# Twelve of sixteen score products ahead of V, and two-row runs for wo's heads 24 to 29, in a gated mix of cached attention and a SwiGLU block

## The chip, the cores and the metric

The kernel runs on one core of a Trainium2 chip. The core has a matrix engine (TensorE, PE in the profile; its weight loads are PEld), a vector engine (VectorE, DVE), a scalar engine (ScalarE, ACT), a general engine (GpSimd, POOL) and a sync engine (SyncE, SP), which here issues nearly all transfers. Sixteen DMA engines move data between the memory of the chip and the core's on-chip memory. The metric is the device time of one execution in microseconds (us), as a median of several runs.

## The reference

One token is decoded. `x` has 512 numbers; there are 32 heads of 128 numbers, each with a cache of 65,536 keys and as many values, all in bf16.

```
q = (x @ wq) as 32 heads of 128
scores = einsum(q, k_cache) * 128 ** -0.5
p = softmax(scores)
o = einsum(p, v_cache)
a = o as 4096 numbers @ wo                     # wo: 4096 x 512
b = (silu(x @ w_gate) * (x @ w_up)) @ w_down   # 512 -> 1792 -> 512
g = sigmoid(sum(x * gate_w))
out = g * a + (1 - g) * b
```

The two caches are 537 MB each, and every byte of them is read once.

## The kernel before

**Tiles.** A tile is 128 x 128 cache rows, that is 128 partitions with `NB` = 128 rows each; rows have 128 numbers. Two tiles are a pair (64 KB a partition, 8.39 MB). A head has four tiles (`G`), two pairs (`MH`), so there are 128 tiles (`N`) and 64 pairs (`M`). There are two buffers for K pairs (`K_bufs`, a half for each tile) and one for V (`V_buf`).

**A step.** Step `m` handles K pair `m` and V pair `m-2`. A step with an even `m` is the first of a head's two, one with an odd `m` the second (`second` in the matrix engine's code, `b == 1` elsewhere).

- *Vector engine* (`vector_step`, L342). `product` (L279) multiplies the pair's first tile by the query in place. `add_once` (L309) adds the upper 64 numbers of each row to the lower 64 and raises the credit `c_S[0]`. Then comes the maximum of the previous head (`top_of`, L330) or the fold of the tile before. The second tile is multiplied, and `add_halves` (L291) adds halves down to 16 numbers, the last of them into `T_sb`, and raises `c_S[1]`. Just ahead of that last add it folds the pair's first tile: `fold` (L320) sums four columns of the score accumulator `S_ps` into `S_sb`, after waiting for the matrix engine's event `pe_S`. In a second step the other tile's fold and the row maximum (`row_max`, L326) follow.
- *Matrix engine* (`tensor_step`, L683). It takes credits, each raised by another engine, in a fixed order. `take(c_S[0])`, then 16 products of the 64 remaining columns with a unit matrix, four columns each, which accumulate into `S_ps[0]` (`scores`, L513). Then `c_P` (probabilities are ready; first steps only, in second steps it is taken ahead of the scores) and `c_V` (the V pair has landed). Then 64 products of probabilities with V into `O_ps` (`values`, L537), 32 for each tile, each tile ending with the event `pe_V`. Then the sum of the exponentials (`total`), the next query's spread (`query_spread`, L527), `c_S[1]` and the four scores of the second tile out of `T_sb`, the turn of `O_sb` (`head_turn`, L545) and the turn of the maximum (`max_turn`, L530). The first matrix product on `T_sb` raises `pe_K`, which frees the K pair.
- *Scalar engine* (`scalar_step`). It forms the exponentials into `P_sb`, copies `O_ps` out (`o_copy`), scales a head's output into `oT` (`head_out`) and copies the new query.
- *Sync engine* (`sync_step`, L214). It waits for `pe_V`, issues the next V pair's load (L181), waits for `pe_K` and issues the load of a K pair (L181). GpSimd passes on that V has landed, as the credit `c_V` (`tell_of_v`).

Steps 2 to 61 are loops on the matrix engine (two steps an iteration, 30 iterations), the vector engine (four steps) and the scalar engine (four heads, up to `GROUPED`). The last two K pairs are written out; there the scores of both tiles are 16 products, and `add_halves` stops at 64 columns.

**The end.** `sync_end` (L220) issues the last V tiles in pieces and then `wo` (`load_wo`, L187) into the first K buffer, in the pieces of `WO_CUTS`. The first 28 heads (`GROUPED`) are loaded so that a partition takes four rows of `wo` that lie side by side, a run of 4 KB; the other heads take a run of 1 KB for each head. Because of that order, `o_copy` writes a head's output in a regrouped order and `head_out` puts it into `oT` in four pieces of 32 partitions. `project` (L551) multiplies `oT` by `wo` head by head, two products a head, waiting for each piece of `wo`. The two halves of the result are then copied out by the vector and the scalar engine (L388, L392), and 1 KB is written back (L237).

Of the kernel before, what the change touches and what calls it, by code (L numbers as in the profile page):

```python
# [10 lines left out]
P = 128  # L11
NB = 128
PAIR = 2 * NB
QUAD = 4


WIDE = 64
WIDTH = 16

TURNED = 8  # L20
WO_CUTS = (0, 4, 8, 12, 16, 20, 24, 28, 30, 31, 32)
HALVES = (0, 64, NB)
LAST_CUTS = (0, 32, 64, 96, 112, NB - TURNED, NB)

GROUPED = 28


class Events:
# [12 lines left out]
def kernel(  # L41
# [18 lines left out]
    _, H, Sk, Dh = A_k_cache.shape  # L60
# [17 lines left out]
    def sb(name, shape, dtype=f32):  # L78
        return consts.tile(shape, dtype, name=name)
# [10 lines left out]
    O_sb = sb("O_sb", [4, 4 * Dh])  # L90
# [3 lines left out]
    ident_b, ones_b, q_diag = (sb(n, [P, P], bf16) for n in ("ident_b", "ones_b", "q_diag"))  # L94
# [3 lines left out]
    oT = sb("oT", [P, H], bf16)  # L98
# [12 lines left out]
    S_ps = [psum.tile([P, NB, QUAD], f32, name=f"S{i}_ps") for i in range(2)]  # L111
    O_ps = psum.tile([4, 4 * Dh], f32, name="O_ps")
# [13 lines left out]
    def halves(buf):  # L126
        return [buf[:, i * NB * Dh : (i + 1) * NB * Dh].rearrange("p (j d) -> p j d", d=Dh) for i in range(2)]

    K_half, V_half = [halves(b) for b in K_bufs], halves(V_buf)

    wo_sb = K_bufs[0][:, : H * D].rearrange("p (h n) -> p h n", n=D)

    def v_view(n):
        return {N - 4: K_half[0][1], N - 3: V_half[0], N - 2: V_half[1], N - 1: K_half[1][1]}[n]

    sync, act, dve, pool, pe = nc.sync, nc.scalar, nc.vector, nc.gpsimd, nc.tensor
# [3 lines left out]
    po, pe_x, pe_S, pe_V, pe_q, pe_m, pe_t, pe_o = (  # L140
        Events(nc, n) for n in ("po", "pe_x", "pe_S", "pe_V", "pe_q", "pe_m", "pe_t", "pe_o")
    )
# [9 lines left out]
        for n in ("x_in", "gw_in", "wq_in", "ka_in", "kb_in", "kc_in", "wg_in", "wu_in", "wd_in", "vA_in", "vB_in")  # L152
# [4 lines left out]
              for n, c in ((N - 3, HALVES), (N - 2, HALVES), (N - 1, LAST_CUTS))}  # L157
    wo_in = {a: Events(nc, f"wo{a}", 16) for a in WO_CUTS[:-1]}

# [7 lines left out]
    def wait(engine, events, value):  # L167
        key = id(engine), id(events)
        value -= taken.get(key, 0)
        if seen.get(key, 0) < value:  # L170
            engine.wait_ge(events.sem, value)
            seen[key] = value
# [10 lines left out]
    def load_tile(view, cache, n, events, a=0, b=NB):  # L183
        start = n % 2 * NB
        events(sync.dma_start(out=view[:, a:b, :], in_=rows_of(cache, n)[:, start + a : start + b, :]))  # L185

    def load_wo(a, b):  # L187
        runs = wo_sb.rearrange("p (g j) n -> p g (j n)", j=QUAD)
        rows = A_wo.rearrange("(h p) n -> p h n", p=P)
        row_runs = A_wo.rearrange("(g p j) n -> p g (j n)", p=P, j=QUAD)  # L190
        if b <= GROUPED:
            A, B = a // QUAD, b // QUAD
            wo_in[a](sync.dma_start(out=runs[:, A:B, :], in_=row_runs[:, A:B, :]))  # L193
        else:
            wo_in[a](sync.dma_start(out=wo_sb[:, a:b, :], in_=rows[:, a:b, :]))


    def load_v(i):
# [21 lines left out]
    def sync_end():  # L220
        wait(sync, pe_D, 6)
        load_tile(v_view(N - 4), A_v_cache, N - 4, v4_in)
        for n in (N - 3, N - 2, N - 1):
# [5 lines left out]
            for events, a, b in zip(end_in[n], cuts[:-1], cuts[1:]):  # L229
                load_tile(v_view(n), A_v_cache, n, events, a, b)  # L230
        for a, b in zip(WO_CUTS[:-1], WO_CUTS[1:]):
            load_wo(a, b)
# [45 lines left out]
            wait(dve, ac_q, n // G)  # L278
        return own[0](dve.tensor_tensor(out=K, in0=K, in1=q_rep, op=ALU.mult))  # L279

    def add_halves(n, width, last, out=None, ahead=None):
        K = K_half[n // 2 % 2][n % 2]
        half, mark = Dh // 2, last
        while half >= width:
            wait(dve, own[0], mark)
            to = K[:, :, 0:half]
            if half == width and ahead is not None:
                fold(ahead)
            if half == width and out is not None:
                to = out  # L290
            ins = dve.tensor_tensor(out=to, in0=K[:, :, 0:half], in1=K[:, :, half : 2 * half], op=ALU.add)  # L291
            if half == width and out is not None:
                ins.then_inc(c_S[n % 2], 1)
            else:
                mark = own[0](ins)
            half //= 2
        marks["K", n] = mark
# [16 lines left out]
    def fold(n):  # L314
        h, g = divmod(n, G)
        if n < G or n >= N - G:
            wait(dve, pe_D, n + 1 if n < G else n + 1 - N + 2 * G)
        else:
            wait(dve, pe_S, n + 1 - G)
        return own[0](dve.tensor_reduce(  # L320
            out=S_sb[h % 2][:, g * NB : (g + 1) * NB], in_=S_ps[n % 2], axis=AXIS.X, op=ALU.add
        ))
# [19 lines left out]
    def vector_step(m):  # L342
        h, b = divmod(m, MH)
        width, to = (WIDTH, T_sb) if m < M - 2 else (WIDE, None)
        last = product(2 * m)
        if to is not None:
            add_once(2 * m, last)
        if b == 0:
            top_of(h - 1)
        else:  # L350
            fold(2 * m - 1)
        if to is None:
            add_halves(2 * m, width, last)
        last = product(2 * m + 1)
        if b == 1:
            weight(h - 1, m - 1)
        add_halves(2 * m + 1, width, last, to, 2 * m)
        if b == 1:
            row_max(h, fold(2 * m + 1))

# [39 lines left out]
    def at(tile, first, i):  # L400
        return tile[:, first + i : first + i + 1] if isinstance(first, int) else tile[:, bass.ds(first + i, 1)]
# [19 lines left out]


    def o_copy(h):
        if h >= GROUPED:
            return copy(O_sb, O_ps)
        return copy(
            O_sb.rearrange("q (c j a) -> q c a j", c=4, j=QUAD),
            O_ps.rearrange("q (c a j) -> q c a j", c=4, j=QUAD),
        )


    def head_out(h, src, first=0):
        wait(act, dv_rg, h + 1)
        if h >= GROUPED:
            return copy(oT[:, h : h + 1], src, rg[:, h % 2 : h % 2 + 1])
        g, part = divmod(h, QUAD)
        A = P // QUAD
        for j in range(QUAD):
            ins = copy(
                at(oT[part * A : (part + 1) * A, :], first, g * QUAD + j),  # L440
                src[j * A : (j + 1) * A, :],
                rg[j * A : (j + 1) * A, h % 2 : h % 2 + 1],
            )
        return ins
# [42 lines left out]
    def scalar_end():  # L487
        took_rounds(act, scalar_waits, GROUPED // QUAD)
        for m in range(2 + GROUPED * MH, M):
            scalar_step(m)  # L490
# [17 lines left out]
        pe.wait_ge(credit, 1)  # L508
        pe.sem_inc(credit, -1)  # L509

    def scores(n, src, width, events, start=0, stop=NB):
        for c in range(0, width, QUAD):
            ins = pe.matmul(  # L513
                S_ps[n % 2][:, start:stop, :], lhsT=ident_b, rhs=src[:, start:stop, c : c + QUAD],
                start=(c == 0), stop=(c == width - QUAD),
            )
            if c == 0 and events is pe_S and n == 1:
                pe_K(ins)
        if stop == NB:
            events(ins)  # L520
# [14 lines left out]
    def values(probs, view, start, stop, opens, closes):  # L535
        for j in range(start, stop, 4):
            ins = pe.matmul(  # L537
                O_ps, lhsT=probs[:, j : j + 4], rhs=view[:, j : j + 4, :],
                start=(opens and j == start), stop=(closes and j == stop - 4),
            )  # L540
        return ins
# [141 lines left out]
    def tensor_step(m):  # L683
        second = m % MH
        if second:
            take(c_P)
            total()
        take(c_S[0])
        scores(0, K_half[m % 2][0], WIDE, pe_S)
        if not second:  # L690
            take(c_P)
        take(c_V)
        for i in range(2):
            pe_V(values(P_sb[:, i * NB :], V_half[i], 0, NB, i == 0, i == 1))
        if not second:
            total()
        take(c_q)
        query_spread(pe_q)
        take(c_S[1])
        scores(1, T_sb, WIDTH, pe_S)  # L700
        take(c_o)
        head_turn()
        take(c_m)
        max_turn()


    def tensor_end():
# [31 lines left out]
        for n in range(N - 3, N):  # L739
            probs = P_last[:, n % G * NB : (n % G + 1) * NB]  # L740
            cuts = LAST_CUTS if n == N - 1 else HALVES
            for events, a, b in zip(end_in[n], cuts[:-1], cuts[1:]):
                wait(pe, events, 16)
                if n == N - 1 and a == NB - TURNED:
                    break
                ins = values(probs, v_view(n), a, b, False, n == N - 1 and b == NB - TURNED)
            pe_V(ins)
            if n == N - 2:
                total(1)
        wait(pe, ac, marks["oh_read"])  # L750
        for j in range(NB - TURNED, NB):
            pe.matmul(
                oh, lhsT=v_view(N - 1)[:, j, :], rhs=probs[:, j : j + 1],
                start=(j == NB - TURNED), stop=False,
            )
        for a, b in zip(WO_CUTS[:-1], WO_CUTS[1:]):
            wait(pe, wo_in[a], 16)
# [7 lines left out]
    with tc.tile_critical():  # L765
# [6 lines left out]
        sync_out()  # L772
        with act.Fori(0, GROUPED, QUAD) as first:
            scalar_round(first)
# [45 lines left out]
```

## Time and profile before

| What | Value |
|---|---|
| median of 3 runs | 2516.11 us (2516.02 to 2516.18) |
| the profiled execution | 2517.2 us |
| its span, first to last instruction | 2515.4 us |
| mean granted matrix-engine clock | 0.774 of full |
| PE, PEld busy | 1487.4 us (59%), 616.2 us (24%) |
| DVE busy | 2003.4 us (80%) |
| ACT busy | 182.3 us (7%) |
| read from memory | 1087.64 MB, 432 GB/s over the span |

The profile was taken in one execution. Busy times overlap between engines, so they do not add up to the span. "Idle before" a group of instructions names what ended the idleness; PEq is the matrix engine's own sequencer, as when it takes a credit. Times within the span are counted from its first instruction. SPq lines show when the sync engine issued a transfer, not when data moved.

### The profile page before, as it was taken

Reading aid. Unit: us, or ns where it says so; the run is one execution under the profiler, and the core shown is the slowest. Engines: PE = TensorE matmul, PEld = TensorE weight load, DVE = VectorE, ACT = ScalarE, POOL = GpSimd, SP = SyncE. Lnnn points to the kernel's source line nnn. Section 1 sums busy time; section 2 is a strip of 40 time slices with the busy share of each in tenths; the row PEclk is TensorE's granted clock in tenths of the full one; section 3 lists DMA queues with packets and bytes.
Section 4 is the critical chain, followed back from the end, with each engine's and each line's share of the span. In section 5 each row is a group of like instructions: output and inputs, shape, how many; then the busy total and the mean of one; then the engine's idle time right before and its main releaser. Section 6 shows DMA issues by size and latency. Waiting matters only on the chain. (4 is left out here: it accounts for less than half of the span.)

```text
span 2515.4 us, 15705 instructions
## 1 busy us (share of the span) xinstructions
PE 1487.4 (59%) x6589; PEld 616.2 (24%) x6589; DVE 2003.4 (80%) x678; ACT 182.3 (7%) x503; POOL 0.7 (0%) x6
## 2 busy tenths in 40 slices
PE   2655655646556556465575565654745656547569
PEld 1322222222222222222222222222212222222223
DVE  5887887877878878779788788787787887977881
ACT  0000000000000000000000000000000000000000
POOL 0000000000000000000000000000000000000000
PEclk8777878778778777787787777877877778778789
DMA  9999999999999999999999999999999999999999
GB/s 414 438 433 436 435 434 434 434 434 434 435 434 434 434 434 434 435 436 435 435 435 434 437 434 435 435 434 437 435 434 434 434 434 434 434 435 434 434 431 387
DMA packets 22605, 1087.80 MB, mean 432 GB/s; under 512 B 2753, under 2 KB 3266, under 8 KB 4546
## 3 DMA queue, kind: packets, MB, share of 16 engines
q1 hardware_dynamic: 22306, 1087.65, 99.9%
q8 instruction: 7, 0.11, 0.0%
q10 hardware_dynamic: 288, 0.00, 0.0%
q14 instruction: 4, 0.03, 0.0%
HBM read 1087.64 MB, written 0.00 MB: 432 GB/s over the span
## 5 line engine op out<-in xcount | busy, mean ns | idle before, releaser
L279 DVE TENSOR_TENSOR K_buf<-K_buf,q_sb 128x16384 bf16<-128x16384 bf16 (+1 forms) x129 | 1112.0, 8620 | 348.8 <-DMA K_buf<-in_A_k_cache_dram 346.1
L513 PE MATMUL S_ps<-K_buf,ident_b 128*128 128x512 bf16 (+1 forms) x1104 | 388.9, 527 | 867.3 <-PEq L509 834.3
L537 PE MATMUL O_ps<-V_buf,P_sb 128*4 128x512 bf16 x3968 | 866.9, 379 | 28.6 <-PEq L509 28.3
L537 PEld LDWEIGHTS O_ps<-V_buf,P_sb 128*4 128x4 bf16 x3968 | 332.9, 85 | 560.1 <-issue 57.6
L291 DVE TENSOR_TENSOR K_buf<-K_buf 128x4096 bf16<-128x4096 bf16 (+1 forms) x127 | 433.7, 3415 | 3.1
L513 PEld LDWEIGHTS S_ps<-K_buf,ident_b 128*128 128x128 bf16 x1104 | 133.5, 126 | 1101.0 <-issue 1036.8
L309 DVE TENSOR_TENSOR K_buf<-K_buf 128x8192 bf16<-128x8192 bf16 x60 | 265.5, 4425 | 2.0
L392 ACT ACTIVATE O_sb<-O_ps 4x512 f32<-4x512 f32 x63 | 63.3, 1005 | 1705.1 <-PE qm_ps L527 1674.8
L320 DVE TENSOR_REDUCE S_sb<-S_ps 128x128 f32<-128x512 f32 x128 | 88.2, 689 | 105.4 <-PE S_ps L513 103.3
L530 PE MATMUL qm_ps<-diag,ones_f 128*128 128x128 f32 x126 | 33.5, 353 | 72.3 <-PEq L509 70.2
L545 PE MATMUL oh_ps<-ident_f,O_sb 4*128 4x1 f32 x504 | 64.3, 244 | 19.6 <-PEq L509 19.6
L291 DVE TENSOR_TENSOR T_sb<-K_buf 128x2048 bf16<-128x2048 bf16 x60 | 72.9, 1214 | 0.0
L545 PEld LDWEIGHTS oh_ps<-ident_f,O_sb 4*128 4x128 f32 x504 | 60.7, 186 | 49.7 <-issue 49.7
L513 PE MATMUL S_ps<-T_sb,ident_b 128*128 128x512 bf16 x240 | 64.7, 391 | 0.0
L530 PEld LDWEIGHTS qm_ps<-diag,ones_f 128*128 128x128 f32 x126 | 21.6, 215 | 76.3 <-issue 76.3
L392 ACT ACTIVATE bias<-top 128x1 f32<-128x1 f32 x32 | 6.5, 203 | 436.4 <-DVE top L330 436.4
L533 PE MATMUL tot_ps<-rs,ones_f 128*128 128x2 f32 (+1 forms) x126 | 24.8, 266 | 17.6 <-PEq L509 17.5
L392 ACT ACTIVATE oT<-whole_o,rg 32x1 f32 (+1 forms) x115 | 33.8, 294 | 4.7
L417 ACT ACTIVATE P_sb<-S_sb,bias 128x256 bf16<-128x256 f32 x62 | 31.5, 508 | 1.0
L533 PEld LDWEIGHTS tot_ps<-rs,ones_f 128*128 128x128 f32 x126 | 20.3, 202 | 36.5 <-issue 36.5
L513 PEld LDWEIGHTS S_ps<-T_sb,ident_b 128*128 128x128 bf16 x240 | 20.7, 96 | 15.9
L326 DVE TENSOR_REDUCE m<-S_sb 128x1 f32<-128x512 f32 x32 | 22.0, 686 | 1.1
(62 smaller groups left out, 197.1 us busy)
## 6 DMA issues: line engine op xcount, KB each, us to landing
K_buf<-in_A_k_cache_dram SPq DMA_DIRECT2D x4, 4096.0 KB, 32.9
V_buf<-in_A_v_cache_dram SPq DMA_DIRECT2D x2, 4096.0 KB, 21.3
V_buf<-in_A_v_cache_dram SPq DMA_DIRECT2D x4, 2048.0 KB, 17.6
V_buf<-in_A_wq_dram SPq DMA_DIRECT2D x1, 4096.0 KB, 12.3
K_buf<-in_A_v_cache_dram SPq DMA_DIRECT2D x1, 4096.0 KB, 29.9
K_buf<-in_A_wo_dram SPq DMA_DIRECT2D x7, 512.0 KB, 16.8
K_buf<-in_A_v_cache_dram SPq DMA_DIRECT2D x3, 1024.0 KB, 23.5
V_buf<-in_B_w_gate_dram SPq DMA_DIRECT2D x1, 1792.0 KB, 54.4
```

The costliest lines, as they stand in the source:

```text
L279: return own[0](dve.tensor_tensor(out=K, in0=K, in1=q_rep, op=ALU.mult))
L291: ins = dve.tensor_tensor(out=to, in0=K[:, :, 0:half], in1=K[:, :, half : 2 * half], op=ALU.add)
L309: dve.tensor_tensor(out=K[:, :, 0:half], in0=K[:, :, 0:half], in1=K[:, :, half:], op=ALU.add).then_inc(c_S[0], 1)
L320: return own[0](dve.tensor_reduce(out=S_sb[h % 2][:, g * NB : (g + 1) * NB], in_=S_ps[n % 2], axis=AXIS.X, op=ALU.add))
L326: (dv_max if h else dv_first)(dve.tensor_reduce(out=m_sb[:, 0:1], in_=S_sb[h % 2], axis=AXIS.X, op=ALU.max))
L392: return act.activation(out=out, in_=in_, func=ACT.Copy, scale=scale)
L417: return act.activation(out=out, in_=S_sb[h % 2][:, b * PAIR : b * PAIR + count], func=ACT.Exp, bias=bias[:, 0:1], scale=scale, accum_out= ...
L513: ins = pe.matmul(S_ps[n % 2][:, start:stop, :], lhsT=ident_b, rhs=src[:, start:stop, c : c + QUAD], start=(c == 0), stop=(c == width - QUAD),
L530: pe.matmul(mT, lhsT=ones_f, rhs=diag, start=True, stop=True).then_inc(pe_m.sem, n)
L533: pe_t(pe.matmul(tot[:, :n], lhsT=ones_f, rhs=rs[:, :n], start=True, stop=True))
L537: ins = pe.matmul(O_ps, lhsT=probs[:, j : j + 4], rhs=view[:, j : j + 4, :], start=(opens and j == start), stop=(closes and j == stop - 4),)
L545: ins = pe.matmul(oh, lhsT=O_sb[:, c * Dh : (c + 1) * Dh], rhs=ident_f[0:4, c : c + 1], start=(opens and c == 0), stop=(c == 3),)
```

## The change

Three things are changed.

1. In `tensor_step`, twelve of the sixteen wide products (`AHEAD` = 48 columns) stay ahead of the V products, and four move behind them. The event `pe_S` of the first tile comes with the last of the four.
2. In `vector_step`, the fold of the pair's first tile moves from before the last add of the second tile to after it. The two written-out steps at the end use the same code.
3. `GROUPED` goes from 28 to 24. Heads 24 to 29 are loaded in runs of two rows (2 KB) a partition, in three pieces of two heads; heads 30 and 31 stay as they were. `o_copy` and `head_out` follow the new grouping, and the scalar engine's loop covers 24 heads instead of 28, with the other four written out.

```diff
+AHEAD = 48
+
 TURNED = 8
-WO_CUTS = (0, 4, 8, 12, 16, 20, 24, 28, 30, 31, 32)
+WO_CUTS = (0, 4, 8, 12, 16, 20, 24, 26, 28, 30, 31, 32)
...
-GROUPED = 28
+GROUPED = 24
+RUNS = ((0, GROUPED, QUAD), (GROUPED, 30, 2), (30, 32, 1))
+
+
+def run_of(h):
+    return next(r for r in RUNS if h < r[1])
...
     def load_wo(a, b):
-        runs = wo_sb.rearrange("p (g j) n -> p g (j n)", j=QUAD)
-        rows = A_wo.rearrange("(h p) n -> p h n", p=P)
-        row_runs = A_wo.rearrange("(g p j) n -> p g (j n)", p=P, j=QUAD)
-        if b <= GROUPED:
-            A, B = a // QUAD, b // QUAD
-            wo_in[a](sync.dma_start(out=runs[:, A:B, :], in_=row_runs[:, A:B, :]))
-        else:
-            wo_in[a](sync.dma_start(out=wo_sb[:, a:b, :], in_=rows[:, a:b, :]))
+        base, end, run = run_of(a)
+        runs = wo_sb[:, base:end, :].rearrange("p (g j) n -> p g (j n)", j=run)
+        rows = A_wo[base * P : end * P, :].rearrange("(g p j) n -> p g (j n)", p=P, j=run)
+        A, B = (a - base) // run, (b - base) // run
+        wo_in[a](sync.dma_start(out=runs[:, A:B, :], in_=rows[:, A:B, :]))
...
-    def add_halves(n, width, last, out=None, ahead=None):
+    def add_halves(n, width, last, out=None):
...
-            if half == width and ahead is not None:
-                fold(ahead)
...
-        add_halves(2 * m + 1, width, last, to, 2 * m)
+        add_halves(2 * m + 1, width, last, to)
+        fold(2 * m)
         if b == 1:
             row_max(h, fold(2 * m + 1))
...
     def head_out(h, src, first=0):
         wait(act, dv_rg, h + 1)
-        if h >= GROUPED:
+        base, _, run = run_of(h)
+        if run == 1:
             return copy(oT[:, h : h + 1], src, rg[:, h % 2 : h % 2 + 1])
-        g, part = divmod(h, QUAD)
-        A = P // QUAD
-        for j in range(QUAD):
+        g, part = divmod(h - base, run)
+        A = P // run
+        for j in range(run):
...
-    def scores(n, src, width, events, start=0, stop=NB):
-        for c in range(0, width, QUAD):
+    def scores(n, src, width, events, start=0, stop=NB, ahead=0):
+        for c in range(ahead, width, QUAD):
...
         take(c_S[0])
-        scores(0, K_half[m % 2][0], WIDE, pe_S)
+        K = K_half[m % 2][0]
+        for c in range(0, AHEAD, QUAD):
+            pe.matmul(S_ps[0], lhsT=ident_b, rhs=K[:, :, c : c + QUAD], start=(c == 0), stop=False)
         if not second:
             take(c_P)
         take(c_V)
         for i in range(2):
             pe_V(values(P_sb[:, i * NB :], V_half[i], 0, NB, i == 0, i == 1))
+        scores(0, K, WIDE, pe_S, ahead=AHEAD)
         if not second:
             total()
```

More of the change, by code (lines that the diff above doesn't have):

```diff
@@ L423, in o_copy @@
     def o_copy(h):
-        if h >= GROUPED:
+        run = run_of(h)[2]
+        if run == 1:
             return copy(O_sb, O_ps)
         return copy(
-            O_sb.rearrange("q (c j a) -> q c a j", c=4, j=QUAD),
-            O_ps.rearrange("q (c a j) -> q c a j", c=4, j=QUAD),
+            O_sb.rearrange("q (c j a) -> q c a j", c=4, j=run),
+            O_ps.rearrange("q (c a j) -> q c a j", c=4, j=run),
         )
@@ L433, in head_out @@
         wait(act, dv_rg, h + 1)
-        if h >= GROUPED:
+        base, _, run = run_of(h)
+        if run == 1:
             return copy(oT[:, h : h + 1], src, rg[:, h % 2 : h % 2 + 1])
-        g, part = divmod(h, QUAD)
-        A = P // QUAD
-        for j in range(QUAD):
+        g, part = divmod(h - base, run)
+        A = P // run
+        for j in range(run):
             ins = copy(
-                at(oT[part * A : (part + 1) * A, :], first, g * QUAD + j),
+                at(oT[part * A : (part + 1) * A, :], first, base + g * run + j),
                 src[j * A : (j + 1) * A, :],
```

## The prediction

> **What bounds the kernel now.** I began with the slices and the DMA part of the page, because the kernel reads 1087.64 MB and does little arithmetic per byte.
>
> ```profile
> DMA  9999999999999999999999999999999999999999
> GB/s 414 438 433 436 435 434 434 434 434 434 435 434 434 434 434 434 435 436 435 435 435 434 437 434 435 435 434 437 435 434 434 434 434 434 434 435 434 434 431 387
> ```
>
> All 40 slices have the DMA engines at 90% or more, and outside the first and the last slice the rate stays within 431 to 438 GB/s. Windows of 400 us between 150 and 2150 us give a DMA share of 1.00 each, at 434 or 435 GB/s. At that rate 1087.65 MB take about 2505 us of the 2515.4 us span, so some 10 us at the two ends are not streaming. The list of waits then says whether an engine delays the stream.
>
> ```profile
> ACT O_sb L392 <- PE qm_ps L527: 1674.8, 61, 35.7
> ...
> DVE K_buf L279 <- DMA K_buf<-in_A_k_cache_dram: 346.1, 63, 22.8
> ...
> PE O_ps L537 <- PEq L509: 28.3, 41, 1.3
> ```
>
> DVE waits for a K pair 63 times, 346.1 us in all, so K arrives last, not DVE. The short third wait (L509, the `take` of a credit) stands ahead of the first V product: PE has finished its scores and waits for the credit that says that V has landed. The same cycle in order of time, PE, then DVE, then the load queue:
>
> ```profile
> 1219.71 5.77 PE L513 MATMUL S_ps<-K_buf,ident_b 128*128 128x512 bf16 x16 [14.56 <-PEq L509]
> 1225.87 13.97 PE L537 MATMUL O_ps<-V_buf,P_sb 128*4 128x512 bf16 x64 [0.38 <-PEq L509]
> 1239.77 0.23 PE L527 MATMUL qm_ps<-q_diag,ones_b 128*128 128x128 bf16 x1
> 1239.84 1.08 PE L513 MATMUL S_ps<-T_sb,ident_b 128*128 128x512 bf16 x4
> ```
> ```profile
> 1240.96 0.69 DVE L320 TENSOR_REDUCE S_sb<-S_ps 128x128 f32<-128x512 f32 x1 [3.21 <-PE S_ps L513]
> 1241.68 0.69 DVE L326 TENSOR_REDUCE m<-S_sb 128x1 f32<-128x512 f32 x1
> 1245.01 8.69 DVE L279 TENSOR_TENSOR K_buf<-K_buf,q_sb 128x16384 bf16<-128x16384 bf16 x1 [2.64 <-DMA K_buf<-in_A_k_cache_dram]
> ```
> ```profile
> 1239.87 0.33 SPq L181 DMA_DIRECT2D V_buf<-in_A_v_cache_dram  x1
> ```
>
> The last V product frees the V buffer, and at 1239.87 the next V load is issued. The K pair in flight lands at 1245.01, so the load stands in the queue 5.14 us before its turn. Over the 60 such V loads that lead is 4.79 to 5.17 us, once 5.81. K pairs land 38.6 to 38.7 us apart (1206.42, 1245.01, 1283.69), which is 16.78 MB at 434 GB/s. So the stream never runs dry, and the engines fit inside its period: DVE has 2.64 us left in a step that ends a head (row maximum) and 8.1 us in the other.
>
> At the end:
>
> ```profile
> 2508.23 1.03 PE L554 MATMUL a_ps<-K_buf,oT 128*1 128x256 bf16 x8 [0.21 <-DMA K_buf<-in_A_wo_dram]
> 2509.48 1.03 PE L554 MATMUL a_ps<-K_buf,oT 128*1 128x256 bf16 x8 [0.21 <-DMA K_buf<-in_A_wo_dram]
> 2510.73 1.91 PE L554 MATMUL a_ps<-K_buf,oT 128*1 128x256 bf16 x16 [0.21 <-DMA K_buf<-in_A_wo_dram]
> ```
> ```profile
> DMA to landing us min/median/max: 13.2/13.4/13.6
> ```
>
> The second fence is the answer for line L195, the loads of heads 28-29, 30 and 31; the last is issued at 2498.9, so it lands near 2512.1. Four heads of wo land every 1.25 us. After heads 24 to 27 land, PE runs 16 products back to back and ends at 2512.64, half a microsecond behind the last landing.
>
> **Scores 12 and 4.** Nothing is added or removed: 16 products a step before and after, in 60 steps. Four warm products cost 4 x 0.218 = 0.87 us (13.97 us for 64 matmuls of this width). PE now reaches the V credit that much earlier, but V has not landed: in the step shown PE already waited 0.38 us, elsewhere up to 1.26. Where scores run cold all through (6.57 us at 678.79) V begins straight after them; there it may begin some 0.3 us earlier. So V ends where it ended, or 0.3 us earlier, and the V load with it. Worth to the stream: 0, since its engines are already full. If that cover went, the price of a late V load would be its lateness beyond the lead, step by step.
>
> The 0.87 us move behind V. Late by that are: the query product and its copy on ACT (q is ready near 1242, needed at 1245.01), the narrow scores, the turn of O, the maximum's turn, and `pe_K`, whose K load goes to the queue behind a V load of 19.3 us. None has less than 2 us in hand.
>
> **The fold.** It moves behind the last add and, since the scores now end behind V, it becomes a wait. At 1235.92 it ran for 0.69 us without waiting; after the change it cannot start before 1239.84 + 0.87 + about 0.25 = 1240.95. Queued behind it on DVE are the second fold, the row maximum and the next product. The second fold moves from 1240.96 to about 1241.85, the maximum ends near 1243.3 instead of 1242.37, and DVE still waits 1.7 us for K at 1245.01, against 2.64. In the other kind of step it is free near 1280.2, 3.5 us ahead of K at 1283.69. Cost 0. In the last two steps, written out, the last add before the final scores starts 0.6 us earlier; the transfers behind it are queued some 10 us deep, so 0 as well.
>
> **The clock.** PE now idles between product 12 and V. In the step at 794.66, 16 scores took 4.98 us; 12 take 4.98 - 0.87 = 4.11, so PE stops at 798.77 and V comes at 800.90: 2.13 us idle. The granted clock in stretches of 3.41 us shows what such a gap can do:
>
> ```profile
> 797.44:800.85 3.41, 2.19 (x10) 1.00 0.76 327
> 800.85:804.26 3.41, 3.36 (x16) 1.00 1.20 519
> ```
> ```profile
> 1241.19:1244.60 3.41, 1.16 (x9) 1.00 0.93 404
> 1244.60:1248.01 3.41, 0.51 (x2) 0.50 0.98 423
> ```
>
> With 2.19 us of work in the stretch the clock stayed full, with 1.16 it fell to half in the next. The step at 794.66 would have 1.32, nearer to the row that fell. V would then run at half clock for up to 3.4 us and end 1.7 us late. The phase of the stretches wanders over the steps, so I take it for up to a third of them. The lead of the V load falls from 5.1 to 3.4 us there. What lead is needed? The kernel's first load was issued at 0.96, and data moves in the window 2.00 to 2.50: 1.0 to 1.5 us. So the stream still does not see it. Value taken: 0; kept for the range: a longer drop (below). The Trainium skill, "TensorE: Matmul & The Clock Gate", section "Part 1: The HAM clock gate", gives the gate a free-running window of about 3.4 us, and its section "HAM oscillation — how this bites in real kernels" asks only that no idle gap exceed that. By that rule a gap of 2.1 us keeps the clock and the lead stays at 5.1; the trace's 1241.19 stretch, which fell without a 3.4 us gap, speaks against relying on it. The sum is 0 by both, but by the rule the slow rival would have no chance.
>
> **wo.** Heads 24 to 27 (512 KB) go from one DMA of 4 KB runs to two of 2 KB runs, heads 28-29 from 1 KB to 2 KB runs: one more DMA. 512 KB take 1.25 us in 4 KB runs (landings above) and 2512.1 - 2510.68 = 1.42 us in 1 KB runs; 2 KB lies between, which no row shows: 0 to +0.17 on heads 24 to 27, -0.09 to 0 on 28-29. Middle: about +0.04. The extra issue takes 0.5 us on SP, which issues 13 us ahead. After the wait for heads 26-27 (near 2510.75) 12 products of 0.119 us are left instead of 16, so PE is no longer behind; it ends two products and one pipeline depth after the last landing, 2512.1 + 0.05 + 0.12 + 0.27 = 2512.55 against 2512.64. Gain 0.1 us, bounds 0.5 (four products of heads 24-25 wholly hidden, landing 0.4 us earlier) and -0.2. The outputs' copies for heads 24 to 27 are two instead of four (0.29 us each on an engine 7% busy), those of 28 and 29 two instead of one: 0.
>
> **Sum.** Loop 0, folds 0, wo -0.1. The profiled execution has a span of 2515.4 us and took 2517.2, so 1.8 lie around the span; it becomes 2515.3 and 2517.1. The runs' median 2516.11 is 1.1 below that execution; the same difference gives **2516.0**.
>
> **The rivals.**
> *V starts cold for longer, and the stream runs dry (slower).* For it: 16 scores at 2447.09 never left half clock in 6.48 us. Over such a length V ends 3.2 us late, the lead is 1.9 us, minus 0.9 if DVE and thus the scores slip too: 1.0. It decides once the lead falls below the 1.0 to 1.5 us that the first load needed. Price: up to 0.5 us in a third of 60 steps, 10 us: 2526. Against it: wherever PE was busy through a whole stretch, the clock rose, and V is a dense 14 us.
> *An earlier V load quickens the stream (faster).* For it: steps alternate 38.59 and 38.68 us. If all were 38.59, 30 x 0.09 = 2.7 us: 2513.4. Against: DMA share 1.00 at any lead from 4.79 to 5.81.
> *The last loads get worse.* If heads 24 to 29 in 2 KB runs moved like the 1 KB ones and the extra DMA's issue of 0.5 us came to stand in the way: +0.17 + 0.5, 2516.7. The Trainium skill, "DMA: Bandwidth & Descriptors", section "Rules for kernel authors", wants 1 MiB per DMA; by it smaller cuts are a loss. Here 512 KB pieces land at 419 GB/s, so their start-up is already hidden.
>
> **Chances.** Forecast 0.84; last loads worse 0.08; dry stream 0.05; quicker stream 0.03. The measurement can tell 0.2%, 5 us, from no change. Only the dry stream passes that: slower 0.05, faster 0.01 (something unseen), same 0.94. The range takes 2515.0 from the best wo bound with the runs' own scatter and a part of the quicker stream, and 2518.0 above for worse last loads and a few dry steps.
>
> **What would show it.** V's first product still 0.2 us after V lands, with a longer wait at the credit (1.2 to 2.3 us instead of 0.2 to 1.3); a DVE wait for PE ahead of the first fold in every step, and the wait for K shorter by 1 to 5 us; K landings still 38.6 us apart; V bursts of up to 15.7 us in some steps. If V loads are issued less than 2 us ahead of K's landing, or the rate in a middle slice falls below 430 GB/s, the forecast is wrong.

## The result, and the profile after

The changed kernel is slower: 2524.2 us as the median of 10 runs, against 2516.31 us for the kernel before in its own 10. The ratio is 1.003, with a 95% interval of 1.0022 to 1.0038. It also scatters: 2519.47 to 2530.08 us, where the kernel before stays within 2516.02 to 2517.5. The profiled execution took 2530.08 us, with a span of 2528.3.

The DMA line of the page still shows nine tenths or more everywhere. The rate line below it (GB/s in 40 slices) does not:

```profile
DMA  9999999999999999999999999999999999999999
GB/s 413 438 432 440 432 433 429 435 430 432 431 434 431 430 432 431 434 428 427 433 431 434 432 437 431 423 430 430 432 433 431 432 431 431 428 433 431 432 431 384
```

Before, the inner slices held 431 to 438 and 21 of the 38 were 434. Now 32 are between 428 and 434, and two fall to 427 and 423. The share of busy DMA engines hides a loss of half a per cent; the rate shows it. The waits (engine and line, what it waited for, us in total, times, longest) say who has become late:

```profile
DVE S_sb L322 <- PE S_ps L518: 293.9, 92, 6.8
...
DVE K_buf L283 <- DMA K_buf<-in_A_k_cache_dram: 162.2, 55, 23.0
PE O_ps L542 <- PEq L514: 92.2, 62, 2.4
```

The fold in the kernel before:

```profile
DVE S_sb L320 <- PE S_ps L513: 103.3, 32, 3.7
```

Two things were foreseen: the fold now waits for PE (92 times and 293.9 us instead of 32 times and 103.3), and PE waits longer for the credit of V (92.2 instead of 28.3). But DVE waits for K 55 times instead of 63: in six of the other steps V was long, the folds behind it were late, and DVE took K up 0.2 to 0.5 us after it had landed; in two it came just in time. Two steps in a row, PE first (start, length, then the instruction, in brackets the idle time before it) with the V products of a third, then DVE at K and the V loads:

```profile
1106.57 4.08 PE L696 MATMUL S_ps<-K_buf,ident_b 128*128 128x512 bf16 x12 [12.22 <-PEq L514]
1112.78 15.61 PE L542 MATMUL O_ps<-V_buf,P_sb 128*4 128x512 bf16 x64 [2.13 <-PEq L514]
1128.31 1.04 PE L518 MATMUL S_ps<-K_buf,ident_b 128*128 128x512 bf16 x4
...
1145.22 5.21 PE L696 MATMUL S_ps<-K_buf,ident_b 128*128 128x512 bf16 x12 [12.18 <-PEq L514]
1152.66 15.66 PE L542 MATMUL O_ps<-V_buf,P_sb 128*4 128x512 bf16 x64 [2.23 <-PEq L514]
...
1192.79 13.97 PE L542 MATMUL O_ps<-V_buf,P_sb 128*4 128x512 bf16 x64 [1.97 <-PEq L514]
```
```profile
1131.92 8.69 DVE L283 TENSOR_TENSOR K_buf<-K_buf,q_sb 128x16384 bf16<-128x16384 bf16 x1 [1.85 <-DMA K_buf<-in_A_k_cache_dram]
```
```profile
1128.41 0.33 SPq L188 DMA_DIRECT2D V_buf<-in_A_v_cache_dram  x1
...
1168.35 0.33 SPq L188 DMA_DIRECT2D V_buf<-in_A_v_cache_dram  x1
```

After 12 scores PE is idle for 2.13 us, and then V takes 15.61 us instead of 13.97. The next V load goes out at 1128.41. The K pair in flight is taken up by DVE at 1131.92, so the lead is 3.5 us instead of 5.1. The following V burst starts 39.88 us after this one instead of 38.6, and is long too; the one after it starts 40.13 us later. Against 38.65 us each, those two steps lose 2.7 us. The granted clock in stretches of 3.41 us (the columns are stretch, length, busy PE time with the number of matmuls, clock, DMA share, GB/s) shows why V was long:

```profile
1109.32:1112.73 3.41, 1.32 (x6) 0.99 0.76 327
1112.73:1116.15 3.42, 3.38 (x9) 0.51 1.15 498
1116.15:1119.56 3.41, 3.41 (x17) 1.00 0.97 423
```

The stretch with the gap held 1.32 us of work, and the next one had half the clock, just when V began. The page's group of V products carries the sum of such bursts:

```profile
L542 PE MATMUL O_ps<-V_buf,P_sb 128*4 128x512 bf16 x3968 | 891.6, 386 | 92.2 <-PEq L514 92.2
```

It was 866.9 us before. The extra 24.7 us are 15 bursts at 1.65 us each, and in the order of time 15 of the loop's 60 bursts are 15.5 to 15.7 us long, the other 45 are 13.97. From the first burst of the loop (104.84) to the last (2397.54) lie 2292.7 us, against 2280.1 before: 12.6 of the 12.9 us by which the span grew. That is 0.84 us for a long burst on average, but they are not alike: behind ten of the 15 the next V load landed 0.4 to 1.5 us late, behind five it did not.

The end behaved as forecast. PE at `project`, after the change:

```profile
2521.28 1.03 PE L559 MATMUL a_ps<-K_buf,oT 128*1 128x256 bf16 x8 [0.27 <-DMA K_buf<-in_A_wo_dram]
2522.51 2.99 PE L559 MATMUL a_ps<-K_buf,oT 128*1 128x256 bf16 x24 [0.19 <-DMA K_buf<-in_A_wo_dram]
```

PE ends 0.44 us after the last landing of `wo` (2525.05), before 0.58 us after it (2512.05). From the first product with `wo` to the end of the span it took 11.98 us (2516.28 to 2528.26), before 12.12 (2503.29 to 2515.41): 0.14 us gained.

### The profile page after: what moved, and what is told of

The parts are those of the page before. It is cut to its first block, busy times and chain, and to the rows that moved or that the text cites. A ratio compares the mean times of both kernels' runs of the same rounds, so it can differ in the third digit from the quotient of the medians.

```text
span 2528.3 us, 15610 instructions
## 1 busy us (share of the span) xinstructions
PE 1500.6 (59%) x6589; PEld 617.2 (24%) x6589; DVE 2009.1 (79%) x678; ACT 182.8 (7%) x497; POOL 0.7 (0%) x6
## 5 line engine op out<-in xcount | busy, mean ns | idle before, releaser
L542 PE MATMUL O_ps<-V_buf,P_sb 128*4 128x512 bf16 x3968 | 891.6, 386 | 92.2 <-PEq L514 92.2
L696 PE MATMUL S_ps<-K_buf,ident_b 128*128 128x512 bf16 x720 | 288.4, 579 | 767.1 <-PEq L514 767.1
L542 PEld LDWEIGHTS O_ps<-V_buf,P_sb 128*4 128x4 bf16 x3968 | 338.2, 86 | 654.5 <-issue 168.2
L322 DVE TENSOR_REDUCE S_sb<-S_ps 128x128 f32<-128x512 f32 x128 | 88.2, 689 | 293.9 <-PE S_ps L518 293.9
L696 PEld LDWEIGHTS S_ps<-K_buf,ident_b 128*128 128x128 bf16 x720 | 91.1, 133 | 934.6 <-issue 927.6
L518 PE MATMUL S_ps<-K_buf,ident_b 128*128 128x512 bf16 (+1 forms) x384 | 101.2, 400 | 36.4 <-DVE K_buf L293 26.3
L518 PEld LDWEIGHTS S_ps<-K_buf,ident_b 128*128 128x128 bf16 x384 | 33.8, 103 | 98.2 <-issue 37.9
L395 ACT ACTIVATE oT<-whole_o,rg 32x1 f32 (+2 forms) x109 | 32.0, 294 | 4.3
```

What stands on the lines that cost most here:

```text
L322: return own[0](dve.tensor_reduce(out=S_sb[h % 2][:, g * NB : (g + 1) * NB], in_=S_ps[n % 2], axis=AXIS.X, op=ALU.add))
L395: return act.activation(out=out, in_=in_, func=ACT.Copy, scale=scale)
L518: ins = pe.matmul(S_ps[n % 2][:, start:stop, :], lhsT=ident_b, rhs=src[:, start:stop, c : c + QUAD], start=(c == 0), stop=(c == width - QUAD),
L542: ins = pe.matmul(O_ps, lhsT=probs[:, j : j + 4], rhs=view[:, j : j + 4, :], start=(opens and j == start), stop=(closes and j == stop - 4),)
L696: pe.matmul(S_ps[0], lhsT=ident_b, rhs=K[:, :, c : c + QUAD], start=(c == 0), stop=False)
```

## The experiments

The theory under test is called G: the gap ahead of V lets the clock fall, V is long, its buffer comes free late, the next V load has too little lead, and the stream loses. The rivals were D, the fold that now waits on DVE, and W, the new loads and grouping of `wo`.

**Undoing one part.** *e1_all_ahead* puts all 16 products ahead of V again and keeps the fold's place and `wo`:

```diff
-        for c in range(0, AHEAD, QUAD):
-            pe.matmul(S_ps[0], lhsT=ident_b, rhs=K[:, :, c : c + QUAD], start=(c == 0), stop=False)
+        scores(0, K, WIDE, pe_S)
...
-        scores(0, K, WIDE, pe_S, ahead=AHEAD)
```

> The changed kernel with all 16 wide products ahead of V again; the fold stays behind the last add and wo stays as changed. Theory G (the gap of about 2 us ahead of V lets the clock fall, V then takes 15.6 us instead of 13.97, its next load is issued 3.5 us ahead instead of 5.1 and the stream loses about 1 us each time): no gap, no long V, 2516.2 us. Rival D (the fold, now a wait for scores behind V, makes DVE late for the next K): the fold no longer waits, so also about 2516. Rival W (the loads of wo or the scalar engine's new grouping cost the time): still 2519 to 2530.

Measured: 2516.42 us against 2516.32 (ratio 1.000, 0.999 to 1.0009); no long burst; first product with `wo` to the end 11.99 us. So it is the split that makes the difference, by the gap or by the fold that then has to wait; neither the fold's place by itself nor `wo` costs anything.

*e2_wo_undone* keeps split and fold:

```diff
-WO_CUTS = (0, 4, 8, 12, 16, 20, 24, 26, 28, 30, 31, 32)
+WO_CUTS = (0, 4, 8, 12, 16, 20, 24, 28, 30, 31, 32)
...
-GROUPED = 24
-RUNS = ((0, GROUPED, QUAD), (GROUPED, 30, 2), (30, 32, 1))
+GROUPED = 28
+RUNS = ((0, GROUPED, QUAD), (GROUPED, 32, 1))
```

> The changed kernel with wo's loads and grouping as before (heads 0 to 27 in runs of four rows). Theories G and D: 2519 to 2530 us, as the changed kernel. Rival W: 2516.

Measured: 2526.67 us (ratio 1.0044, 1.0027 to 1.0061), with 10 long bursts in the profiled run of 2526.62. W falls.

**Gap or fold.** *e3_filled_gap* leaves everything as changed and gives PE something to do ahead of V, on the bank that V's first product clears anyway:

```diff
+        for c in range(0, 16, QUAD):
+            pe.matmul(O_ps, lhsT=ident_b[:, 0:4], rhs=K[:, :, c : c + QUAD], start=True, stop=True)
         if not second:
             take(c_P)
         take(c_V)
```

> The changed kernel with four extra products of the width of V's, whose result nobody reads, between the twelve scores and V: they fill 0.87 us of the gap, as the four scores did before. The four scores stay behind V and the fold waits as in the changed kernel. Theory G: no V burst over 14.1 us in the loop, V loads issued 5 us ahead again, 2516 to 2517 us. Rival D: the fold waits as long as in the changed kernel, so 2519 to 2530.

Measured: 2516.36 us (ratio 1.000, 0.9991 to 1.001). Its waits and its V products:

```profile
DVE S_sb L322 <- PE S_ps L518: 261.6, 92, 4.7
DVE K_buf L283 <- DMA K_buf<-in_A_k_cache_dram: 184.1, 63, 23.1
```
```profile
L542 PE MATMUL O_ps<-V_buf,P_sb 128*4 128x512 bf16 x3968 | 866.8, 379 | 27.4 <-PEq L514 26.7
```

The fold waits nearly as long as in the changed kernel, 261.6 us, and DVE has nearly as little to spare, but it waits for K 63 times again. The kernel does more work and is 8 us faster than the changed one. D falls.

*e4_four_left_out* is the counterpart: gap, but no fold that waits.

```diff
-        for c in range(0, AHEAD, QUAD):
-            pe.matmul(S_ps[0], lhsT=ident_b, rhs=K[:, :, c : c + QUAD], start=(c == 0), stop=False)
+        scores(0, K, AHEAD, pe_S)
...
-        scores(0, K, WIDE, pe_S, ahead=AHEAD)
```

> The changed kernel without the four wide products behind V (the last 16 of the 64 columns of the first tile are left out of the scores in the loop's steps): the gap ahead of V stays, the fold no longer waits for V, and the K pair is freed as early as before. Theory G: V bursts of 15.6 us in 10 to 20 of 60 steps and 2519 to 2530 us. Rival D: 2516.

Measured: 2521.77 us, 2518.54 to 2533.38 (ratio 1.0027, 1.0015 to 1.0038). The profiled run, 2521.03 us, had 7 long bursts, fewer than the 10 to 20 expected. Less work than in the kernel before, and still slower. The fold waits 110.2 us here, near the 103.3 of the kernel before.

**How long a gap.** *e8_fourteen* and *e9_eight* change one number, `AHEAD`, to 56 and to 32.

> The changed kernel with 14 wide products ahead of V and two behind. The gap ahead of V is about 1.7 us at most. In e6_tiles_split no gap was over 1.9 us and no V burst was long. Theory G: no long burst, 2516 to 2517 us, although the fold still waits for products behind V. If the loss grows with the number of products moved: about 2520.

> The changed kernel with eight wide products ahead of V and eight behind. The gap ahead of V grows from about 2 to about 3 us. Theory G: hardly a stretch of 3.41 us around the gap then holds enough work, so nearly every V burst is long (50 to 60 of 60), and the loss grows far out of proportion, to 2560 to 2600 us. If the loss only grows with the number of products moved: about 2532.

Measured: 14 ahead 2516.23 us (ratio 0.9999, 0.9989 to 1.0008), no long burst, the longest wait for V's credit 1.8 us. Eight ahead 2546.55 us (1.0113, 1.0097 to 1.013), 50 long bursts of 15.2 to 16.9 us in the profiled run of 2550.18 us. The threshold and the growth out of proportion are there (0, 8 and 30 us for two, four and eight products moved), but the size expected for eight was too large: a long burst cost some 0.6 us here, not 1. The trace shows that most lost nothing: behind 30 of the 50 the next V load landed as usual, 19.3 to 19.6 us after K, though its lead had shrunk to between 2.3 and 4.0 us. Behind the other 20 it landed up to 2.8 us late.

**The lead by itself.** *e5_freed_late* starts from the kernel before, keeps every product where it was, and only frees the V buffer later, at the first product of O's turn:

```diff
-            pe_V(values(P_sb[:, i * NB :], V_half[i], 0, NB, i == 0, i == 1))
+            ins = values(P_sb[:, i * NB :], V_half[i], 0, NB, i == 0, i == 1)
+            if i == 0:
+                pe_V(ins)
...
-        head_turn()
+        head_turn(freed=pe_V)
```

> The kernel before, where in the loop's steps the event that frees the V buffer is raised by the first product of O's turn instead of by the last V product, about 1.4 us later; all products stay in their order, so the clock has no reason to change. V loads are then issued about 3.7 us ahead of K's landing instead of 5.1. Theory G: the lead alone costs the time; from the changed kernel, where steps with 3.5 us of lead were followed by about 0.9 us of loss, 60 such steps give 2550 to 2585 us with no V burst over 14.1 us. The prediction's own reading (a lead of 1.0 to 1.5 us is enough): 2516.

Measured: 2581.52 us (1.0261, 1.0244 to 1.0278). The V load goes out 2.0 us after the last V product instead of 0.03. One step of it, the load, PE, and two windows (stretch, length, busy time of PE, PEld, DVE, ACT and POOL with instructions, clock, DMA share, GB/s):

```profile
1234.84 0.33 SPq L181 DMA_DIRECT2D V_buf<-in_A_v_cache_dram  x1
```
```profile
1251.72 4.99 PE L513 MATMUL S_ps<-K_buf,ident_b 128*128 128x512 bf16 x16 [15.01 <-PEq L509]
1258.83 13.97 PE L537 MATMUL O_ps<-V_buf,P_sb 128*4 128x512 bf16 x64 [2.12 <-PEq L509]
```
```profile
1235.00:1240.00 5.00, 1.30 (x9) 0.99 (x8) 1.57 (x1) 0.99 (x4) 0.00 (x0) 0.75 0.87 315
1240.00:1245.00 5.00, 0.00 (x0) 0.00 (x0) 5.00 (x1) 0.00 (x0) 0.00 (x0) 0.50 0.95 406
```

The window that begins with the V load's issue in the kernel before:

```profile
1240.00:1245.00 5.00, 2.48 (x15) 1.54 (x12) 1.38 (x2) 2.99 (x8) 0.00 (x0) 0.96 0.97 419
```

V products run at their normal 13.97 us in 57 of 60 steps, and still the bursts are 39.75 us apart on average, 1.1 us more than before. Three bursts were long (15.39 to 15.66 us), where none was expected; V had come so late that PE stood idle for 2.1 to 2.6 us ahead of it. They are too few for the 65 us lost. At 1238.42 DVE takes up K, 3.6 us after the V load was issued, and around that moment the DMA engines move 315 GB/s. From the issue of the load to the first V product are 24.0 us in this step; in the kernel before it was 24.6, so 1.5 us less lead brought only 0.6 us. A short lead thus costs time without long bursts; that is shown. It does not cost it every time: with leads of 3.0 to 4.0 us, 16 of these 57 V loads landed without delay.

*e11_freed_mid* frees the buffer about halfway, at the third narrow product (`if c == 2 * QUAD`).

> As e5_freed_late, but the V buffer is freed by the third narrow product, about 0.8 us after V, so that V loads are issued about 4.35 us ahead of K's landing. e5_freed_late issued V about 1.9 us later than the kernel before and lost 1.1 us a step, so some 0.8 us of the lead was spare. Theory: a spare of 0.8 us takes this delay, 2516 to 2522 us. If every microsecond of lateness costs a microsecond: 0.8 x 60, about 2562.

Measured: 2531.44 us (1.0065, 1.0048 to 1.0082), but from 2518.67 to 2536.62. The profiled run was the one at 2518.67; its leads are mostly 4.1 to 4.3 us, and its bursts are 38.67 us apart. So one execution bears a lead of 4.1 to 4.3 us; the other three, of which there is no trace, took 2529.79 to 2536.62 us. Neither expectation was met, and it stays open what tips an execution over. One trace can only hint at it: in the good execution the sixteen DMA engines ended a K load closer together than in the kernel before, mostly within 0.9 us instead of 1.9, so the first of them came to the V load 2.9 us after its issue, as late as before.

**Long bursts without a short lead.** *e6_tiles_split* and *e7_tiles_before* load each V pair as two tiles, the first as soon as its half of the buffer is free:

```diff
-            wait(sync, pe_V, 2 * i)
-            load_pair(V_buf, A_v_cache, i, vA_in)
+            for n in (2 * i, 2 * i + 1):
+                wait(sync, pe_V, n - 1)
+                load_tile(V_half[n % 2], A_v_cache, n, (vA_in, vB_in)[n % 2])
...
```

The credit `c_V` then waits for both tiles.

> The changed kernel, where each V pair is loaded as two tiles, each as soon as its own half of the buffer is free: the first tile's load is issued some 7 us earlier, when half of V's products are done. Its runs are 32 KB instead of 64 KB. Theory G: V bursts of 15.6 us remain, but cost nothing, since the lead is 10 us and more; the time is that of the kernel before with the same loads (e7_tiles_before) within 2 us. If long V bursts cost time otherwise than by the lead: 4 to 12 us above e7_tiles_before.

> The kernel before, where each V pair is loaded as two tiles, each as soon as its own half of the buffer is free; the control for e6_tiles_split. All theories: 2516 us plus what runs of 32 KB cost in place of 64 KB, 2516 to 2521.

Measured: 2518.5 and 2518.69 us (1.0008 and 1.0009), so loading in two tiles with runs of 32 KB costs 2.2 to 2.3 us. But e6 proves nothing on the lead: the longest wait for V's credit was 1.9 us, and not one burst was long. *e12_tiles_eight* takes the tiles to eight products ahead.

> e9_eight with V loaded as two tiles, each as soon as its own half of the buffer is free (e6_tiles_split had the tiles, but lost its long V bursts, so it did not test this). The gap stays at 2 to 3 us, so long V bursts come back in most steps; the first tile's load is issued some 7 us earlier. Theory G: long bursts without loss, within 2 us of e7_tiles_before, 2517 to 2521 us. If long bursts cost time otherwise than by the lead of the V load: 2540 to 2550, as e9_eight.

Measured: 2518.51 us (1.0008, 0.9998 to 1.0017), like its control, 28 us faster than eight ahead without the tiles. One step of it, PE and the two loads of the V pair ahead:

```profile
1220.42 3.57 PE L698 MATMUL S_ps<-K_buf,ident_b 128*128 128x512 bf16 x8 [12.75 <-PEq L516]
1226.60 15.66 PE L544 MATMUL O_ps<-V_buf,P_sb 128*4 128x512 bf16 x64 [2.62 <-PEq L516]
```
```profile
1195.07 7.23 SPq L192 DMA_DIRECT2D V_buf<-in_A_v_cache_dram  x2
```

V takes 15.66 us as in the changed kernel; in all, 48 of the 60 bursts are over 14.6 us. The first tile's load is issued at the middle of the burst, 9.3 us or more ahead of K's landing, and nothing is lost. In half of the steps DVE takes K up 0.5 to 2.3 us after its landing here, so a DVE late by that much costs nothing either. Long bursts hurt only through the lead of the next V load.

No version beat the kernel before: e8_fourteen and e3_filled_gap equal it.

## Why the prediction was wrong

*What bounds the kernel*: right. The stream of K and V bounds both kernels, and the loop, which streams them, lost 12.6 of the 12.9 us.

*Scores 12 and 4*: right that V cannot start earlier, since it starts when it has landed; right about the longer wait at the credit.

*The fold*: right. It became a wait in every step, and e3 and e8, where it waits 261.6 and 234.5 us, show that it costs nothing. DVE's 1.7 us in hand at K were 1.8; a long V burst uses them up, which the prediction did not add.

*The clock*: right in mechanism and nearly in size. 1.32 us of work in the stretch with the gap was the estimate, 1.32 is what the stretch at 1109.32 holds. V 1.7 us late was the estimate, 1.65 was measured; "up to a third" of the steps, 15 of 60 were, among them the step that it took as its example (V now at 802.22). That the 1.32 agree to the digit is luck, since the stretches lie differently in every step. The lead falls to 3.4 us was the estimate, 3.5 was measured.

*"What lead is needed? ... 1.0 to 1.5 us"*: this is the step that failed, and with it "the stream still does not see it" and the value 0. The figure was taken from the kernel's first load, the time from its issue until data moves. With leads of 3.4 to 3.8 us ten of the changed kernel's 15 late V loads landed 0.4 to 1.5 us late, and with leads mostly of 3.0 to 4.0 a step of e5 lost 1.1 us. With 4.1 to 4.3 some executions lost time (e11), with the 4.8 and more of the kernel before no load came late. A fixed least lead is not shown, since some loads with 2.5 us came in time (e9).

Two things separate the first load from one in the stream, and the packets in the trace of the changed kernel show both. The lead was counted to K's landing, but the sixteen engines do not end K together. In this loop they end it over 1.3 to 3.0 us, so behind the long bursts the first engine came to the V load 0.6 to 2.1 us after its issue, not 3.4 to 3.8. And packets that begin so soon after the issue are slower. In the loop of the kernel before, 26 of the 15,102 packets of 64 KB took over 2.45 us, where 2.42 is the usual; now 723 of 15,104 did. The time beyond the usual comes to 10.1 us for each of the sixteen engines, instead of 0.6, three quarters of it in packets that begin within 5 us after a V load's issue. So of the 12.6 us lost some 9.5 are slower packets, and the remaining 3 or so are engines without work. Why such packets are slower stays open.

The trace of before held a warning that was not used: no V load in the loop had less than 4.79 us of lead, so everything under that was unmeasured, and a lead of 3.4 us was priced by a row from another situation.

*The slow rival* named the right mechanism and set its deciding point at the same 1.0 to 1.5 us, so it had a chance of 0.05 only, and its price of 0.5 us in a third of the steps needed a longer cold spell than occurred. An ordinary spell of one stretch was enough. It also argued that wherever PE was busy through a whole stretch the clock rose. At the start of the kernel before, two stretches from 63.57 to 70.40 are busy throughout and stay at 0.50. One of the prediction's own signs of being wrong appeared: five middle slices fell below 430 GB/s, one to 423.

*The rule on idle gaps* in "TensorE: Matmul & The Clock Gate" (Trainium skill, section "HAM oscillation — how this bites in real kernels"), by which gaps under 3.4 us keep the clock, did not hold: gaps of 2.0 to 2.4 us lost it. With the same page's free-running window of 3.4 us, in its section "Part 1: The HAM clock gate", the trace agrees: its clock changes in stretches of 3.41 us.

*wo*: right, in mechanism too. PE has less left behind the last landing; 0.1 us gain was the forecast, 0.14 was measured, and no median can show it.

## What to carry to other kernels

In a kernel that streams without a gap, look for the transfer that is issued last before its turn and treat its lead as the budget; the smallest lead that the trace shows to be harmless throughout is the only proven one, and the start-up of a first transfer is no measure of it. Work taken out of a wait makes an idle gap, and the gap can cost more than the work: here four products that seemed to lengthen the path kept the clock up for the 64 behind them. If a buffer comes free late, freeing and loading it in halves takes the lead out of danger (e12), for 2.3 us of shorter runs and more loads here.

## What was not expected of the hardware

- The matrix engine's clock can fall over a gap of 2 us, if the stretch of 3.41 us around it holds little work. In the three traced kernels that do twelve products ahead of V and nothing more, all 32 V bursts behind a gap of 1.98 us or more were long, and none behind a shorter one. The length of the gap alone does not decide: in e5, with all 16 ahead, 17 of 20 gaps of that length kept the clock.
- The stretches run free of the program, so where a gap falls in one differs from step to step. The runs of the split kernels scatter by 4 to 15 us, with 15, 10 and 7 long bursts in profiled runs of 2530.08, 2526.62 and 2521.03 us; the kernel before, e1 and e8 stay within 2.1 us.
- A shorter lead did not bring a load of 8.39 MB in by as much sooner: in e5 it landed 23.9 us after its issue (median) with 3.4 us of lead, in the kernel before 24.4 with 5.1. The transfer itself is 19.3 of these.
- The DMA share read 0.99 to 1.01 in the loop's windows of 50 us of the kernel before, and the slices of the slower kernel still read 9 throughout: half a per cent is visible only in the rate.
